# Crossing the row halves of half of the heads in a fused attention and expert kernel

## The chip, the cores and the metric

The kernel runs on one core of a Trainium2 chip. The metric is the device time of one execution in microseconds. A core has five engines with queues of their own: TensorE (PE) multiplies matrices and writes its results to PSUM banks, VectorE (DVE), ScalarE (ACT) and GpSimd (POOL) work element by element, and SyncE (SP) issues the transfers here. PE alone writes banks; POOL doesn't read them.

## The reference

Attention with gates, a recurrence over 768 steps for 2 batches of 8 heads with 40 channels each, and behind it two expert layers:

```
m_new = max(f_gate[t] + m, i_gate[t])
f, i  = exp(f_gate[t] + m - m_new), exp(i_gate[t] - m_new)
C = f * C + i * outer(v[t], k[t])          # per head 40 x 40
n = f * n + i * k[t]
y[t] = sigmoid(o_gate[t]) * (C @ q[t]) / max(|n . q[t]|, 1)
...
x1 = ((x @ w_a) * (x @ w_b)) @ w_out       # 1536 x 320, inner 1536
x2 = leaky(x1 @ w_in) @ w_out2             # inner 2048, slope 0.01
```

Inputs of the attention are single precision; the weights come as double precision and are decoded on the chip.

## The kernel before, in words

The recurrence is worked out in six chunks of 128 steps (`p` from 0 to 5) for each batch (`b`), and each chunk in two halves of 64 steps (`c`). On the partitions lie the 128 steps of a chunk; 64 u and up are the heads 4u to 4u+3 where channels lie on the partitions. For each (p, b) PE makes

- `dmm` (`decay_mm`, L341): the decays of chunk 0 and 1 spread over the partitions,
- `smm` (`score_mm`, L379): keys times queries, 16 small matmuls,
- `stm` (`state_mm`, L493): keys times values, 16 small matmuls, emptied by `ste` (L506, L508),
- `av` (`value_mm`, L436): scores times values, 32 matmuls of 64 rows by 32 columns,
- `qc` (`query_mm`, L450): queries times state, 16 matmuls of 64 by 64, onto the same two banks,
- `xmm` (L519): the transposes to the layout of the expert layer.

Each matmul in single precision is two instructions in the trace. Between them stand DVE (`dsc` the scan of the decays, L354; `sat` scores times decays, L385; `ste`; `onm`, `nrm`), POOL (`val`, `vo` values times gate; `key`; `qry`; `stk` the fading state, L499; `og`), and ACT (`sig` the sigmoid, `oab`, `nd`, `xh`). The small results (`pa`) have two banks, the `up` results (`mm`) two, the `dn` results four, which `p` = 0 borrows for scores and outputs.

The first expert layer runs on blocks of 256 tokens (blocks 0 and 1) and of 512 (2 and 4). `up` (`up_mm`, L592) is 16 matmuls, `dn` (`down`, L650 to L652) is three for each 128 tokens. Between them stand `e1`, `em`, `eh`, `el` on ACT and DVE. Each of 18 pieces of its weights (`lw:0` to `lw:17`, 640 or 768 KB) is loaded into one of four tiles `y`, then decoded by `dh` and `dl` (ACT), `dm` (DVE), `dr` (ACT, rounded part) and `ds` (POOL, L249, L250, L259, remainder), which frees the tile. Two pieces of every three are for `up`, one for `dn`.

In what order the engines get their instructions is written out by hand: the text `ORDER` lists the steps by name (`up:0:3` is block 0, slice 3; `av:1:1` is p = 1, b = 1), and each step queues its instructions, transfers too, on its engines. An engine works its queue in that order and waits where an operand isn't there or a buffer isn't free. `spin` is a matmul whose result nobody reads. `ca` closes the attention's buffers; behind it come block 4 and the second expert layer (`um`, `dd`, `ym`).

Gates: `gs` is the scan for m, `gi`, `gfa`, `gfb` the differences, `gei`, `gef`, `gst` the exponentials, `gist` the transpose of the input gate to columns, `gcum` a scan of the decays inside a chunk. `sdec` and `scum` store decays in DRAM, and `lf` and `ld` load them back, spread over partitions.

Some lines that count:

```
at_t: scores, [128 (half c on partitions 64c and up), 4 heads, 64]
ps[u]: output bank of heads 4u to 4u+3, partitions = steps
value_mm:  ps[u][x, i] += at_t[p, b, u][64 c ..., i, x] . v[64 c ..., 4 u + i]   with u = (j // 4 + c) % 2
query_mm:  ps[u][64 c ..., i] += qs[64 u ..., i, 64 c ...] . state_c[64 u ..., i]
```

Of the kernel before, what the change touches and what calls it, by code (L numbers as in the profile page):

```python
# [23 lines left out]
NP = 6  # L24
T = 128
# [8 lines left out]
    lg:0 lc:0 init lw:0 lk:0:0 gs:0 spin gi:0 gfa:0 gei:0 gfb:0 spin lg:1 gst:0 gef:0 dh:0 gz:0 gs:1 gfa:1 spin idr  # L34
    spin dl:0 gfb:1 ls:0:0 gist:0 dmm:0:1 dmm:0:0 gi:1 gcum:0 lk:0:1 gs:2 spin ls:0:1 gi:2 smm:0:0 dsc:0:1 val:0:0
    gfa:2 scum:0 gei:1 key:0:1 dm:0 val:0:1 dsc:0:0 sat:0:0:0 lw:1 vo:0:1 stm:0:1 gst:1 gef:1 vo:0:0 dr:0 sig:0:0
    key:0:0 sat:0:0:1 gz:1 smm:0:1 ld:0:1 ste:0:1:0 stm:0:0 ld:0:0 sig:0:1 ds:0 dh:1 gfb:2 lw:4 sat:0:1:0 qry:0:1
    sat:0:1:1 av:0:1 gcum:1 av:0:0 dl:1 ste:0:0:0 dm:1 qc:0:1 dr:1 stk:0:1:1 qry:0:0 dh:4 oab:0:1 onm:0:1 dl:4
    qc:0:0 oab:0:0 ste:0:1:1 lw:2 nrm:0:1 onm:0:0 stk:0:0:1 dl:2 scum:1 dh:2 gst:2 dmm:1:0 lk:1:0 lw:5 nrm:0:0 gef:2
    dm:2 ds:1 gist:1 ld:1:0 spin spin spin gei:2 og:0:1 og:0:0 nd:0:0 ste:0:0:1 val:1:0 spin lw:3 dr:2 xmm:0:0  # L40
    ls:1:0 dsc:1:0 nd:0:1 lk:2:1 dm:4 spin xmm:0:1 lk:1:1 key:1:0 xh:0:0 gz:2 xh:0:1 dr:4 xl:0:0 xl:0:1 spin spin
    spin dh:3 vo:1:0 gist:2 dh:5 ds:2 up:0:0 e1:0:0 lw:6 em:0:0 stk:1:0:0 smm:1:0 sat:1:0:1 dl:3 sat:1:0:0 ds:4 dm:3
    sig:1:1 eh:0:0 dr:3 stm:1:0 spin qry:1:0 ste:1:0:0 lw:7 stk:1:0:1 el:0:0 ste:1:0:1 ls:1:1 dl:5 up:0:1 spin
    av:1:0 qc:1:0 e1:0:1 sig:1:0 dm:5 sdec:2 oab:1:0 val:1:1 dn:0:0 dr:5 nrm:1:0 ld:1:1 dl:6 em:0:1 dh:6 ds:3 vo:1:1
    lw:9 ds:5 onm:1:0 gcum:2 dh:7 dl:7 dmm:1:1 spin up:0:3 dsc:1:1 dm:6 smm:1:1 dr:6 sat:1:1:0 og:1:0 up:0:2 eh:0:1
    sat:1:1:1 key:1:1 lw:8 stk:1:1:0 stm:1:1 dm:7 dr:7 el:0:1 lk:2:0 e1:0:3 ste:1:1:0 dl:9 e1:0:2 ds:6 stk:1:1:1
    nd:1:0 dn:0:1 em:0:3 sig:2:1 ste:1:1:1 ls:2:0 em:0:2 scum:2 lw:10 up:0:4 av:1:1 eh:0:3 eh:0:2 dl:8 qry:1:1 dh:8
    el:0:2 e1:0:4 em:0:4 qc:1:1 ld:2:1 oab:1:1 nrm:1:1 onm:1:1 ds:7 dn:0:2 eh:0:4 og:1:1 dm:8 xmm:1:0 xh:1:0 up:0:5
    nd:1:1 el:0:3 xmm:1:1 ld:2:0 val:2:0 dn:0:3 vo:2:1 xh:1:1 xl:1:0 dh:10 e1:0:5 qry:2:0 lf:2:1 lf:2:0 dr:8
    stk:2:0:0 xl:1:1 up:1:2 em:0:5 dl:10 vo:2:0 eh:0:5 ls:3:0 dh:9 dsc:2:0 key:2:0 el:0:4 e1:1:2 el:0:5 smm:2:0  # L50
    up:1:1 lw:11 sig:2:0 em:1:2 sat:2:0:1 up:1:0 dh:11 val:2:1 sat:2:0:0 dm:10 ds:8 lf:3:0 stm:2:0 dm:9 ste:2:0:0
    e1:1:0 em:1:0 ls:2:1 eh:1:2 dr:9 lf:3:1 dn:0:4 dn:0:5 eh:1:0 stk:2:0:1 ste:2:0:1 av:2:0 qc:2:0 el:1:2 stk:2:1:0
    dsc:2:1 e1:1:1 dr:10 nrm:2:0 em:1:1 up:1:5 oab:2:0 key:2:1 eh:1:1 lw:12 smm:2:1 dl:11 dl:12 el:1:1 up:1:3
# [24 lines left out]
    onm:5:1 nrm:5:1 key:5:0 stm:5:0 stk:5:0:0 ste:5:0:0 av:5:0 qc:5:0 em:2:10 oab:5:0 onm:5:0 up:2:11 el:2:9 nrm:5:0
    og:5:0 nd:5:0 og:5:1 nd:5:1 e1:2:11 xmm:5:1 xmm:5:0 xh:5:0 eh:2:10 xh:5:1 dn:2:8 em:2:11 el:2:10 xl:5:0 xl:5:1
    ca lw:19 lw:20 dn:2:9 up:4:0 e1:4:0 dh:19 eh:2:11 lw:21 em:4:0 el:2:11 up:4:1 dn:2:10 dn:2:11 dh:20 eh:4:0 dl:19  # L80
    dl:20 e1:4:1 dm:20 el:4:0 em:4:1 dm:19 eh:4:1 dr:19 up:4:2 e1:4:2 dh:21 dr:20 ye:2 dl:21 ds:19 ds:20 lw:25 lw:18
# [43 lines left out]
def attention_experts_kernel(ctx: ExitStack, tc: tile.TileContext, gates, consts, stk, kvo, w1, wd1, w2, wd2, out):  # L125
# [38 lines left out]
    ct = [[c_p.tile([128, 4, E1], F32, name=f"ct{b}{k}") for k in range(2)] for b in range(B)]  # L164
    cm = [c_p.tile([128, 4, E1], F32, name=f"cm{b}") for b in range(B)]
# [24 lines left out]

    def load_decay_f(p, b):
        t = a_p.tile([128, H, HT], F32, tag="pp", name="pp", bufs=3)
        for c in range(2):
            sp.dma_start(
                out=t[HT * c:HT * c + HT], in_=fdr[2 * p + c, b * H:b * H + H].partition_broadcast(HT)
            )
        p_t[p, b] = t

    def load_decay_c(p, b):
        t = db_free.pop(0)  # L200
        uses["db", p, b] = 2 if p in (0, NP - 1) else 3
        for u in range(2):
            h = b * H + 4 * u
            sp.dma_start(out=t[64 * u:64 * u + D], in_=ddr[p, h:h + 4].partition_broadcast(D))
        db_t[p, b] = t
# [114 lines left out]
    def gate_ist(cc, n):  # L320
        ps = ps_att("mm")
        r = slice(0, B * H)
        for j in range(n):
            pe.transpose(ps[:, j * 16:j * 16 + 16], g_i[r, (cc + j) * T:(cc + j + 1) * T], ident_all[r, 0:16])
        dve.tensor_copy(istn[:, cc:cc + n, :], ps[:, 0:n * 16].rearrange("p (c r) -> p c r", r=16))
# [10 lines left out]
    def decay_mm(p, b):  # L336
        src = ps_att()
        for h in range(H):
            row = b * H + h
            for c in range(2):  # L340
                pe.matmul(  # L341
                    src[HT * c:HT * c + HT, h * HT:h * HT + HT],
# [475 lines left out]
```

## Time and profile before

| what | value |
| --- | --- |
| time of the runs shown, median of 3 | 456.22 us (455.21 to 458.44) |
| the profiled execution, its own time | 456.19 us |
| its span, first to last instruction | 454.4 us |
| mean granted TensorE clock | 0.989 |
| busy PE, DVE, ACT, POOL | 436.2, 189.0, 213.4, 135.7 us |
| instructions of PE | 4238 matmuls and as many weight loads |
| read from and written to HBM | 39.04 and 2.05 MB |

Busy is the time in which an engine has an instruction at work; matmuls overlap, so PE can be busy and yet not at its full pace. The pace is seen in the distance from one matmul's start to the next one's. The span begins with the first instruction; what lies around it, 1.8 us here, belongs to the time but not to the profile.

### The profile page before, as it was taken

How to read it: one execution, taken by the hardware profiler on the slowest of the kernel's cores; microseconds unless marked ns; L12 is line 12 of the kernel's file. 1: busy time of each engine (PE TensorE's matmuls, PEld its weight loads, DVE VectorE, ACT ScalarE, POOL GpSimd, SP SyncE). 2: the span in 40 equal slices, each digit the busy share in tenths (PEclk: the TensorE clock that was granted, in tenths of full speed). 3: DMA queues.
4: the chain of work that ended last, by engine and by line, in shares of the span. 5: the costliest groups of instructions: out<-in, count | busy, mean ns of one | idle time of the engine just before them, and what ended most of it. 6: DMA issues, size and time to landing. Idle time of an engine off the chain costs nothing.

```text
span 454.4 us, 9997 instructions
## 1 busy us (share of the span) xinstructions
PE 436.2 (96%) x4238; PEld 388.6 (86%) x4238; DVE 189.0 (42%) x339; ACT 213.4 (47%) x412; POOL 135.7 (30%) x148
## 2 busy tenths in 40 slices
PE   6599999999999989999999999999999999999996
PEld 4568899998988877788888888989899999899896
DVE  5656687867435322243155431342431131131112
ACT  4687665576323212125676655853443343333222
POOL 6977966767410603010314241020300000000000
PEclk9978999999999999999999999999999999999999
DMA  7897675862311000015422534020010000010001
GB/s 228 272 296 236 237 235 174 270 194 77 112 55 58 1 16 1 1 40 239 138 61 66 178 90 153 0 59 0 1 58 2 0 1 0 1 58 1 0 1 58
DMA packets 12605, 41.74 MB, mean 92 GB/s; under 512 B 1904, under 2 KB 3696, under 8 KB 12560
## 3 DMA queue, kind: packets, MB, share of 16 engines
q1 hardware_dynamic: 12560, 41.10, 28.0%
q8 instruction: 33, 0.54, 0.5%
q14 instruction: 12, 0.10, 0.1%
HBM read 39.04 MB, written 2.05 MB: 90 GB/s over the span
## 4 chain that ended last, share of the span: by engine, by line
PE 84%; DMA 5%; DVE 4%; ACT 2%; issue 2%; POOL 2%; SPq 0%; POOLq 0%; DVEq 0%; ACTq 0%
PE mm L592 26%; PE mm L619 20%; PE dn L650 11%; PE dn L652 10%; PE dn L651 10%; DMA ddr<-wd 2%; DMA stk<-stk 2%; PE pa L436 2%; PE pa L493 1%; PE pa L450 1%; DMA y<-w 1%; PE pa L379 1%; PE pa L682 1%; ACT y L231 1%; PE pa L519 1%
## 5 line engine op out<-in xcount | busy, mean ns | idle before, releaser
L592 PE MATMUL mm<-xh,wa 128*128 128x256 f32 (+1 forms) x480 | 117.3, 345 | 0.6 <-POOL wa L250 0.6
L592 PEld LDWEIGHTS mm<-xh,wa 128*128 128x128 f32 x480 | 80.6, 192 | 9.8 <-POOL wa L250 0.8
L592 PE MATMUL mm<-xl,wa 128*128 128x256 f32 (+1 forms) x288 | 80.0, 339 | 0.0
L635 DVE TENSOR_TENSOR gl<-gg,gh 128x512 fp32r<-128x512 f32 x48 | 34.2, 731 | 99.4 <-ACT gh L630 95.2
L625 ACT ACTIVATE gg<-mm 128x512 f32<-128x512 f32 x48 | 28.1, 593 | 72.3 <-PE mm L619 69.6
L650 PE MATMUL dn<-wa,gh 128*128 128x320 f32 x192 | 59.6, 310 | 0.0
L652 PE MATMUL dn<-wa,gl 128*128 128x320 f32 x192 | 59.4, 309 | 0.0
L651 PE MATMUL dn<-wa,gh 128*128 128x320 f32 x192 | 59.3, 309 | 0.0
L592 PEld LDWEIGHTS mm<-xl,wa 128*128 128x128 f32 x288 | 51.9, 192 | 5.8
L602 DVE TENSOR_TENSOR gg<-gg,mm 128x256 f32<-128x256 f32 (+1 forms) x48 | 26.3, 550 | 66.5 <-PE mm L592 30.4
L597 ACT ACTIVATE gg<-mm 128x256 f32<-128x256 f32 (+1 forms) x48 | 23.2, 486 | 57.3 <-PE mm L592 50.2
L650 PE MATMUL dn<-wd,gh 128*128 128x320 f32 x144 | 46.3, 322 | 0.0
L652 PE MATMUL dn<-wd,gl 128*128 128x320 f32 x144 | 44.6, 309 | 0.0
L651 PE MATMUL dn<-wd,gh 128*128 128x320 f32 x144 | 44.5, 309 | 0.0
L611 DVE TENSOR_TENSOR gl<-gg,gh 128x256 fp32r<-128x256 f32 (+1 forms) x48 | 35.5, 745 | 11.0 <-ACT gh L606 10.6
L630 ACT ACTIVATE gh<-gg 128x512 fp32r<-128x512 f32 x48 | 29.8, 630 | 21.7 <-PE dn L651 21.3
L606 ACT ACTIVATE gh<-gg 128x256 fp32r<-128x256 f32 (+1 forms) x48 | 25.0, 524 | 27.1 <-DVE gg L602 15.8
L651 PEld LDWEIGHTS dn<-wa,gh 128*128 128x128 f32 x192 | 36.1, 188 | 1.2
L650 PEld LDWEIGHTS dn<-wa,gh 128*128 128x128 f32 x192 | 36.1, 188 | 1.2
L652 PEld LDWEIGHTS dn<-wa,gl 128*128 128x128 f32 x192 | 36.0, 188 | 0.0
L619 PE MATMUL mm<-yh,wa 128*128 128x512 f32 x120 | 35.8, 396 | 0.0
L619 PE MATMUL mm<-yh,w 128*128 128x512 f32 x120 | 35.6, 394 | 0.0
(114 smaller groups left out, 702.8 us busy)
## 6 DMA issues: line engine op xcount, KB each, us to landing
y<-w SPq DMA_DIRECT2D x12, 768.0 KB
raw<-w SPq DMA_DIRECT2D x8, 768.0 KB
kvo<-kvo SPq DMA_DIRECT2D x12, 484.0 KB
raw<-wd SPq DMA_DIRECT2D x8, 640.0 KB
stk<-stk SPq DMA_DIRECT2D x24, 160.0 KB
y<-wd SPq DMA_DIRECT2D x6, 640.0 KB
pp<-fdr SPq DMA_DIRECT2D x16, 128.0 KB
db<-ddr SPq DMA_DIRECT2D x24, 80.0 KB
```

The source lines that it names most:

```text
L592: pe.matmul(halves_[ab], w[:, slot, ab, :], xs[lo][:, kt, cs], start=i == 0, stop=i == 7)
L597: act.activation(out=g, in_=up_t[blk, f][0], func=AF.Copy)
L602: dve.tensor_tensor(out=g, in0=g, in1=up_t.pop((blk, f))[1], op=ALU.mult)
L606: act.activation(out=gh, in_=g_t[blk, f], func=AF.Copy)
L611: dve.tensor_tensor(out=gl, in0=g_t.pop((blk, f)), in1=raw_view(gh_t[1, blk, f]), op=ALU.subtract)
L619: pe.matmul(ps, w[:, slot, f % 2, :], xs[lo][:, kt, :], start=i == 0, stop=i == 7)
L625: act.activation(out=g, in_=ps, func=AF.Prelu, alpha=0.01)
L630: act.activation(out=gh, in_=g_t[2, blk, f], func=AF.Copy)
L635: dve.tensor_tensor(out=gl, in0=g_t.pop((2, blk, f)), in1=raw_view(gh_t[2, blk, f]), op=ALU.subtract)
L650: pe.matmul(ps, gh[:, cs], w[:, 0, :], start=f == 0, stop=False)
L651: pe.matmul(ps, gh[:, cs], w[:, 1, :], start=False, stop=False)
L652: pe.matmul(ps, gl[:, cs], w[:, 0, :], start=False, stop=f == last)
```

## The change

Keys and values of the heads 4 to 7 are laid out with the two halves of a chunk swapped on the partitions (on the host, `crossed`); decays, gate columns and scores of these heads follow. Wherever a row half of 64 partitions was half `c`, it is `c ^ u` now. So the value groups can use four different tiles of 64 by 64, and have 16 matmuls in place of 32. Because value and query group then write some of the same places from different row halves, a new step `sy` reads one element of the output bank between them. The gate rows are sorted by (u, b, head), the gate columns come from matmuls with ones on a diagonal in place of transposes, decays are stored with four transfers in place of one, and in the tile `kvo` the output gates stand behind the values. `ORDER` up to `ca` is another; from `ca` on it is the same.

```
-ORDER: lg:0 lc:0 init lw:0 lk:0:0 gs:0 spin gi:0 ... (to ca)
+ORDER: lg:0 lc:0 init gs:0 gi:0 gfa:0 gfb:0 spin gei:0 lk:0:1 ... (to ca)
 loads before:  lg:0 lc lw:0 lk:0:0 lg:1 ls:0:0 lk:0:1 ls:0:1 scum:0 lw:1 ld:0:1 ld:0:0 lw:4 lw:2 scum:1 lk:1:0 lw:5 ld:1:0 lw:3 ls:1:0
 loads after:   lg:0 lc lk:0:1 lk:0:0 lg:1 lw:0 ls:0:1 scum:0 ls:0:0 ld:0:1 lw:1 ld:0:0 lw:2 lk:1:0 scum:1 lw:4 lw:3 ld:1:0 lw:6 ls:1:0
 ACT before:    gei:0 gst:0 gef:0 dh:0 idr dl:0 gei:1 gst:1 gef:1 dr:0 sig:0:0 sig:0:1 dh:1 dl:1 dr:1 dh:4 oab:0:1 dl:4 oab:0:0 dl:2 dh:2
                gst:2 gef:2 gei:2 nd:0:0 dr:2 nd:0:1 xh:0:0 xh:0:1 dr:4 dh:3 dh:5 e1:0:0 dl:3 sig:1:1 eh:0:0 dr:3
 ACT after:     gei:0 gst:0 gef:0 gst:1 gef:1 gei:1 idr dh:0 dl:0 dr:0 gst:2 gef:2 gei:2 sig:0:0 dh:1 dl:1 dl:2 oab:0:0 dr:1 dh:2 sig:0:1
                oab:0:1 sig:1:0 dr:2 dh:4 dl:4 nd:0:0 dh:3 nd:0:1 dr:4 dl:3 xh:0:1 xh:0:0 dl:6 dr:3 dh:6 e1:0:0 e1:0:3 eh:0:0
 PE before:     up:0:0 smm:1:0 stm:1:0 spin up:0:1 spin av:1:0 qc:1:0 dn:0:0 dmm:1:1 spin up:0:3 smm:1:1 up:0:2 stm:1:1 dn:0:1 up:0:4 av:1:1
 PE after:      up:0:0 smm:1:0 up:0:3 stm:1:0 up:0:1 av:1:0 qc:1:0 up:0:2 dn:0:0 stm:1:1 up:0:4 smm:1:1 dn:0:1 av:1:1
 PE before:     smm:5:0 up:2:10 smm:5:1 dn:2:6 stm:5:1 av:5:1 qc:5:1 dn:2:7 stm:5:0 av:5:0 qc:5:0 up:2:11
 PE after:      smm:5:0 dn:2:0 stm:5:0 dn:2:1 av:5:0 up:2:4 qc:5:0 ... smm:5:1 dn:2:3 stm:5:1 dn:2:4 av:5:1 up:2:7 qc:5:1
@@ load_decay_f
-                out=t[HT * c:HT * c + HT], in_=fdr[2 * p + c, b * H:b * H + H].partition_broadcast(HT)
+                out=t[HT * c:HT * c + HT].rearrange("p (u i) t -> p u i t", u=2),
+                in_=fdr[2 * p + c].rearrange("(u b i) t -> b u i t", u=2, b=B)[b].partition_broadcast(HT),
@@ store_decays
-        sp.dma_start(
-            out=fdr[lo // HT:hi // HT].rearrange("c r t -> r c t"),
-            in_=g_e[:, lo:hi].rearrange("r (c t) -> r c t", t=HT),
-        )
+        for c in range(2):
+            src = g_e[:, lo:hi].rearrange("r (p c t) -> r p c t", c=2, t=HT)[:, :, c]
+            to = fdr.rearrange("(p c) r t -> c r p t", c=2)
+            for u in range(2):
+                r = slice(8 * u, 8 * u + 8)
+                sp.dma_start(out=to[c ^ u, r, lo // T:hi // T], in_=src[r])
@@ gate_ist
-            pe.transpose(ps[:, j * 16:j * 16 + 16], g_i[r, (cc + j) * T:(cc + j + 1) * T], ident_all[r, 0:16])
+            t = (cc + j) * T
+            o = ps[:, 32 * j:32 * j + 32]
+            pe.matmul(o[:, 0:16], g_i[:, t:t + T], ident_all[0:B * H, 0:16])
+            for c in range(2):
+                pe.matmul(
+                    o[HT * c:HT * c + HT, 8:24], g_i[:, t + HT * (1 - c):t + HT * (1 - c) + HT],
+                    ident_all[0:B * H, 0:16],
+                )
@@ score_mm, state_mm (r = half(c ^ u)), decay_mm
-                    pe.matmul(sc_t[p, b, u][ts, i * HT:i * HT + HT], x[:, 1, i, ts], x[:, 0, i, ts])
+                    pe.matmul(sc_t[p, b, u][half(c ^ u), i * HT:i * HT + HT], x[:, 1, i, ts], x[:, 0, i, ts])
@@ value_mm
-        for j in range(8):
-            for c in range(2):
-                u, i = (j // 4 + c) % 2, j % 4
-                for w in (2 * c, 2 * c + 1):
-                    x = slice(32 * w, 32 * w + 32)
+        for i in reversed(range(4)):
+            for u in (1, 0):
+                for c in range(2):
+                    r = half(c ^ u)
                     pe.matmul(
-                        ps[u][x, i], at_t[p, b, u][HT * c:HT * c + HT, i, x.start - HT * c:x.stop - HT * c],
-                        v[HT * c:HT * c + HT, 4 * u + i, :],
-                        start=fresh(seen, (u, w)), stop=True, skip_group_check=True,
+                        ps[u][half(c), i], at_t[p, b, u][r, i], v[r, 4 * u + i, :],
+                        start=fresh(seen, (u, c)), stop=True, skip_group_check=True,
                     )
+
+    def rows_apart(p, b):
+        ps, seen = out_banks(p, b)
+        dve.tensor_copy(apart[p * B + b][HT:HT + 1], ps[0][HT:HT + 1, 0, 0:1])
```

The new step's name in `ORDER` is `sy`; on DVE `sy:1:0` stands behind `dm:5`, `sy:0:0` behind `gcum:2`. The exponentials `gst:2 gef:2 gei:2` are those of the gates of the chunks 2 to 5.

## Rows read from the trace of the kernel before

**Rows 1.** The page's first and fourth section: busy time, and the chain by engine.

```profile
PE 436.2 (96%) x4238; PEld 388.6 (86%) x4238; DVE 189.0 (42%) x339; ACT 213.4 (47%) x412; POOL 135.7 (30%) x148
...
PE 84%; DMA 5%; DVE 4%; ACT 2%; issue 2%; POOL 2%; SPq 0%; POOLq 0%; DVEq 0%; ACTq 0%
```

**Rows 2.** Stretches: busy us (instructions) by engine, granted clock, DMA share, GB/s.

```profile
20.00:30.00 10.00, 7.41 (x64) 4.85 (x63) 5.68 (x16) 8.06 (x19) 7.11 (x10) 0.66 0.90 299
...
50.00:60.00 10.00, 9.44 (x159) 8.95 (x158) 5.17 (x14) 6.66 (x18) 9.04 (x11) 1.00 0.59 192
...
36.00:38.00 2.00, 2.00 (x12) 2.00 (x11) 0.90 (x3) 2.00 (x4) 1.60 (x3) 0.53 0.89 354
```

**Rows 3.** The chain that ended last, in order of time: start us, us, what.

```profile
36.12 3.32 PE mm L592 x16
...
42.56 0.85 DVE wd L310
...
53.23 0.74 PE pa L436 x64
53.97 0.61 PE pa L450 x32
...
59.10 1.99 PE mm L592 x16
61.10 0.62 PE pa L379 x32
...
65.75 0.61 PE pa L493 x32
```

**Rows 4.** Timeline of PE, a `dn` and the value group behind it.

```profile
78.51 0.31 PE L651 MATMUL dn<-wd,gh 128*128 128x320 f32 x1
78.66 0.31 PE L652 MATMUL dn<-wd,gl 128*128 128x320 f32 x1
78.90 0.81 PE L436 MATMUL pa<-kvo,at 64*32 64x41 f32 x64
```

**Rows 5.** Timeline of PE: the first `up`, and the last `decay_mm`.

```profile
30.50 0.74 PE L592 MATMUL mm<-xh,wa 128*128 128x256 f32 x4
...
42.19 1.15 PE L341 MATMUL pa<-wd,ident 16*64 16x64 f32 x32
```

**Rows 6.** Groups by line and form: busy us, mean ns, idle us before.

```profile
L227 ACT ACTIVATE y<-y 128x768 f32<-128x768 f32 x12 | 10.9, 916 | 4.1 <-DMA y<-w 4.1
...
L385 DVE TENSOR_TENSOR at<-pa,pp 128x256 f32<-128x256 f32 x20 | 7.7, 416 | 10.3 <-PE pa L379 10.2
```

**Rows 7.** The largest waits of PE, 36 to 205 us: us in total, times, longest.

```profile
PE pa L436 <- DVE cm L508: 1.1, 3, 0.5
PE pa L493 <- DVE at L385: 0.9, 1, 0.9
PE pa L519 <- POOL ya L480: 0.8, 1, 0.8
PE pa L436 <- DVE ct L508: 0.6, 1, 0.6
PE mm L592 <- POOL wa L250: 0.6, 1, 0.6
```

**Rows 8.** Timeline at 164 us: a state's add, and the value group that waits.

```profile
164.30 0.33 DVE L508 TENSOR_TENSOR cm<-pa,cm 128x164 f32<-128x164 f32 x1 [1.37 <-PE pa L493]
...
164.69 0.27 PE L436 MATMUL pa<-kvo,at 64*32 64x41 f32 x4 [0.51 <-DVE cm L508]
```

**Rows 9.** Timeline of SP's queue: the load `ld:1:0`.

```profile
23.60 0.68 SPq L204 DMA_DIRECT2D db<-ddr  x2
```

**Rows 10.** Timeline of ACT in the start-up.

```profile
25.30 1.28 ACT L294 ACT_TABLE_LOAD   x1
...
28.88 0.46 ACT L533 ACTIVATE xh<-pa 128x384 fp32r<-128x384 f32 x1
...
34.58 1.28 ACT L410 ACT_TABLE_LOAD   x1
```

More of the change, by code (lines that the diff above doesn't have):

```diff
@@ L33 @@
 ORDER = """
[L34 to L53, printed above, removed]
@@ L79 @@
-    og:5:0 nd:5:0 og:5:1 nd:5:1 e1:2:11 xmm:5:1 xmm:5:0 xh:5:0 eh:2:10 xh:5:1 dn:2:8 em:2:11 el:2:10 xl:5:0 xl:5:1
-    ca lw:19 lw:20 dn:2:9 up:4:0 e1:4:0 dh:19 eh:2:11 lw:21 em:4:0 el:2:11 up:4:1 dn:2:10 dn:2:11 dh:20 eh:4:0 dl:19
-    dl:20 e1:4:1 dm:20 el:4:0 em:4:1 dm:19 eh:4:1 dr:19 up:4:2 e1:4:2 dh:21 dr:20 ye:2 dl:21 ds:19 ds:20 lw:25 lw:18
+    lg:0 lc:0 init gs:0 gi:0 gfa:0 gfb:0 spin gei:0 lk:0:1 spin spin spin spin gs:1 gst:0 gi:1 lk:0:0 gfa:1 gfb:1
+    spin lg:1 gef:0 gz:0 gst:1 spin lw:0 ls:0:1 gef:1 spin gist:0 spin gcum:0 spin gz:1 val:0:1 gei:1 scum:0 idr
@@ new lines @@
+    val:0:0 ls:0:0 vo:0:1 dh:0 gcum:1 ld:0:1 dmm:0:0 gs:2 lw:1 gfa:2 dsc:0:0 dmm:0:1 dsc:0:1 dl:0 ld:0:0 gist:1 spin
+    key:0:0 smm:0:1 lw:2 lk:1:0 dm:0 key:0:1 vo:0:0 stm:0:1 smm:0:0 gfb:2 sat:0:1:0 sat:0:1:1 av:0:1 dr:0 gst:2 ds:0
+    qry:0:1 gi:2 gef:2 gei:2 gz:2 sig:0:0 sat:0:0:0 stm:0:0 ste:0:0:0 qry:0:0 stk:0:0:1 sat:0:0:1 av:0:0 scum:1
+    ste:0:1:0 gcum:2 lw:4 dmm:1:1 dh:1 dl:1 sy:0:1 stk:0:1:1 sy:0:0 qc:0:0 dl:2 oab:0:0 dm:1 dr:1 dsc:1:1 onm:0:0
+    dh:2 ste:0:1:1 ste:0:0:1 qc:0:1 val:1:0 ds:1 sig:0:1 lw:3 dm:2 nrm:0:0 oab:0:1 ld:1:0 sig:1:0 onm:0:1 dr:2 dh:4
@@ new lines @@
+    lw:6 ls:1:0 gist:2 dmm:1:0 dl:4 ld:1:1 og:0:0 nd:0:0 nrm:0:1 xmm:0:0 spin vo:1:0 spin og:0:1 dm:4 spin dh:3
+    dsc:1:0 ds:2 nd:0:1 lw:5 dr:4 dl:3 spin xmm:0:1 xh:0:1 ds:4 spin dm:3 xh:0:0 dl:6 lk:1:1 lw:7 xl:0:1 dr:3 xl:0:0
+    dh:6 up:0:0 dm:6 smm:1:0 up:0:3 key:1:0 sat:1:0:1 e1:0:0 sdec:2 e1:0:3 scum:2 ds:3 em:0:0 eh:0:0 dr:6 sat:1:0:0
+    stm:1:0 up:0:1 dh:5 stk:1:0:0 qry:1:0 ste:1:0:0 dl:5 stk:1:0:1 ds:6 ls:1:1 el:0:0 em:0:3 ste:1:0:1 key:1:1
+    val:1:1 sig:1:1 dm:5 av:1:0 sy:1:0 dh:7 vo:1:1 lw:11 qc:1:0 eh:0:3 dl:7 el:0:3 e1:0:1 up:0:2 stk:1:1:0 dn:0:0
@@ L164, in attention_experts_kernel @@
     ct = [[c_p.tile([128, 4, E1], F32, name=f"ct{b}{k}") for k in range(2)] for b in range(B)]
+    apart = [c_p.tile([128, 1], F32, name=f"apart{n}") for n in range(NP * B)]
     cm = [c_p.tile([128, 4, E1], F32, name=f"cm{b}") for b in range(B)]
@@ L189, in load_kvo, with row @@
         kvo_t[p, b] = t
+    def row(b, h):
+        return h // 4 * 8 + b * 4 + h % 4
     def load_decay_f(p, b):
@@ L202, in load_decay_c @@
         for u in range(2):
-            h = b * H + 4 * u
-            sp.dma_start(out=t[64 * u:64 * u + D], in_=ddr[p, h:h + 4].partition_broadcast(D))
+            r = row(b, 4 * u)
+            sp.dma_start(out=t[64 * u:64 * u + D], in_=ddr[p, r:r + 4].partition_broadcast(D))
         db_t[p, b] = t
@@ L367, in attention_experts_kernel, with half @@
     sc_t = {}
+    def half(c):
+        return slice(HT * c, HT * c + HT)
     def score_mm(p, b):
@@ L421, in out_banks, with fresh @@
         return [pv for _, _, pv in o_t[p, b]], begun[p, b]
-    def fresh(seen, *keys):
-        new = not seen & set(keys)
-        seen |= set(keys)
+    def fresh(seen, key):
+        new = key not in seen
+        seen.add(key)
         return new
@@ L451, in query_mm @@
                         ps[u][x, i], qs_t[p, b][r, i, x], st[c][r, i, :],
-                        start=fresh(seen, (u, 2 * c), (u, 2 * c + 1)), stop=True, skip_group_check=True,
+                        start=fresh(seen, (u, c)), stop=True, skip_group_check=True,
                     )
@@ L491, in state_mm @@
                 for c in range(n):
-                    r = slice(HT * c, HT * c + HT)
+                    r = half(c ^ u)
                     pe.matmul(ps[c][64 * u:64 * u + 64, i], kvo_t[p, b][r, h * D:h * D + 64], v[r, h, :])
@@ L773 @@
     q, k, v, og = (np.asarray(inputs[n]) for n in ("q", "k", "v", "o_gate"))
-    fg = np.asarray(inputs["f_gate"]).reshape(B * H, S)
-    ig = np.asarray(inputs["i_gate"]).reshape(B * H, S)
+    fg, ig = (
+        np.asarray(inputs[n]).reshape(B, 2, 4, S).transpose(1, 0, 2, 3).reshape(B * H, S) for n in ("f_gate", "i_gate")
+    )
     NC = S // T
@@ L785, in nat, with crossed @@
         return x.reshape(B, H, NC, T, D).transpose(0, 2, 3, 1, 4)
+    def crossed(x):
+        y = nat(x).copy()
+        y[:, :, :, 4:] = np.roll(y[:, :, :, 4:], HT, axis=2)
+        return y
     kvo = np.zeros((B, NC, T, KVO), np.float32)
-    kvo[..., 0:NK] = nat(k).reshape(B, NC, T, NK)
-    kvo[..., NK:2 * NK] = nat(og).reshape(B, NC, T, NK)
-    kvo[..., 2 * NK:].reshape(B, NC, T, H, E1)[..., 0:D] = nat(v)
+    kvo[..., 0:NK] = crossed(k).reshape(B, NC, T, NK)
+    kvo[..., NK + NV:] = nat(og).reshape(B, NC, T, NK)
+    kvo[..., NK:NK + NV].reshape(B, NC, T, H, E1)[..., 0:D] = crossed(v)
     dup = np.concatenate([np.arange(320), np.arange(256, 320)])
```

90 lines of the change are left out of this document (53 added, 37 removed).

## The prediction, made before the changed kernel was run

> **What bounds the kernel now.** I read the page's first sections first: TensorE (PE) is busy for 96% of the span and the chain that ended last is PE for 84% [rows 1]. A busy PE is not a PE at its peak, so I next read stretches of ten microseconds [rows 2]. Between 20 and 30 us PE is busy for 7.4 of 10, while the transfers take 0.90 of the sixteen engines' time; from 60 us on PE waits only briefly [rows 7]. So there are two kernels in one: a start-up in which PE waits for loads, gates and decoded weights, and a long stretch in which it streams expert matmuls. After the step `ca` the order is unchanged, so whatever the change gains or loses before it is carried one to one to the end, as long as PE stays the last to finish.
>
> How fast PE streams comes from the chain in order of time [rows 3]: an `up` of 256 columns takes 1.99 us, a group of scores 0.62, of states 0.61, of values 0.74, of queries 0.61. A `dn` is six matmuls 0.15 apart; where a value group follows, the distance is 0.24, so each entry into such small tiles costs 0.09 us [rows 4]. All this is at the full clock.
>
> How much PE loses in the start-up: `up:0:0` starts at 30.50 [rows 5] and the value group `av:1:1` at 53.23 [rows 3], 22.7 us apart. In between lie five `up` (10.0), two score and two state groups (2.5), a value and a query group (1.35), two `dn` (1.8), a `decay_mm` (1.15, [rows 5]) and five entries (0.45): 17.2 us at full pace. So 5.5 us are lost there. One piece shows: `up:0:1` takes 3.32 instead of 1.99, in a stretch with a granted clock of 0.53, behind waits for scores and states [rows 2, 3]. From 36 to 205 us PE's waits with a named releaser are 4.0 us in their five largest rows [rows 7]; the value groups have 1.7 of it, because they stand right behind state groups, whose two banks must first be emptied.
>
> **The change part by part.**
>
> *Value tiles.* A value group goes from 32 matmuls of 64x32 to 16 of 64x64; each is two instructions in the trace, so 64 become 32. The nearest rows are the query and the state group, which have the form to come: 32 instructions of 64x64 in 0.61 us [rows 3]. That saves 0.74-0.61 = 0.13 us, twelve times: -1.6 us. The bounds are -1.6 and 0 (if the new tiles don't run side by side as those of the query group do).
>
> What speaks against this part: until now, whenever two row halves of the array work at once, they write different banks (scores and queries: bank by row half; states: bank by `c`; values: `u = (j//4+c)%2`). After it both row halves write one bank in neighbouring matmuls, in the value and state groups, though other partitions of it. The Trainium skill has a rule against that (TensorEngine Tiling (Array Packing), Restrictions and Gotchas, the first gotcha): different row tiles cannot access the same PSUM bank at the same time. No row of before can show it; it is a rival below.
>
> *The order on PE.* Before, a query group stands right behind its value group; after, a `dn` or `up` lies between, except for `av:1:0` and `qc:1:0`. From `up:0:0` on I count 27 stretches of small tiles in the old order and 39 in the new one: 12 more entries of 0.09 us [rows 4], +1.1 us (bounds 0 and 2.2). So the first two parts nearly cancel.
>
> *The new wait `sy`.* A VectorE (DVE) copy of one element reads bank 0 after the value group, and the query group may write there only after that. Nothing hides that where `qc` stands directly behind: `av:1:0`. There the copy is queued on DVE behind the merge `dm:5`, which itself waits for ScalarE's (ACT) decode; behind the query group on PE stand all later `up` steps. Elsewhere a `dn` or `up` of 0.9 us or more covers it, which is gone if DVE is late. No such copy is in the trace. The nearest is a value group that waits 0.51 us for a DVE add of 0.33 [rows 8]; without the add's length 0.2 is left. I take 0.7, that round and some 0.5 of a merge that is not done; bounds 0.2 and 4 (a late DVE in half of the chunks).
>
> *Gate columns.* Six transposes become 18 single-precision matmuls, 36 instructions. At `decay_mm`'s 1.15/32 = 0.036 us [rows 5] they are 1.3 us. They lie in the start-up, where PE waits anyway: 0; 1.3 if all of it is on the path.
>
> *Stores and loads of decays.* `sdec` becomes four DMAs, three more issues of 0.34 us on SyncE's (SP) queue, if they cost what the loads of `ddr` do (two in 0.68, [rows 9]); the broadcasts come in pieces half as long. Behind them on SP stand `ls:1:1` and weights that are used later: 0, bounds 0 and 1.
>
> *The start-up order.* All exponentials (`gst:2 gef:2 gei:2`) move ahead of the first sigmoid. So the third and fourth table load, 1.28 us each at 25.30 and 34.58 [rows 10], should go; the one stands ahead of `nd:0:0` and `xh:0:0`, the other ahead of `eh:0:0` and `dr:3`. Against that `dh:3 dl:3` are put ahead of `xh`, two of 0.92 us [rows 6]: together +0.5 us for `xh:0:0`, which is at 28.88 now [rows 10]. And `lw:0` moves from third to sixth among the loads, behind 1.0 MB more, 3.4 us at 299 GB/s [rows 2], which delays the first decode; ACT waited for other things afterwards, so little of it should arrive at `xh`. I let `up:0:0` start where it did, give or take 2 us. What differs is behind it: `up:0:3` follows with its weights decoded, one table load fewer delays `eh:0:0`, `decay_mm` of chunk 1 is already done (1.15 us out of this stretch), and the long scan `gcum:2`, in the chain at 42.56 [rows 3], moves to a time before the first query group. I take 4.0 of the 5.5 us as recovered; bounds: -7.5 (all, and a start 2 us sooner) and +2 (none, and a start 2 us later).
>
> *Waits from 60 to 205 us.* In the new order a `dn` or an `up` lies between state and value group, and between scores and values, in chunks 2 to 5. That takes away the 1.7 us before the value groups and most of the 0.9 before a state group [rows 7]; with the matmuls behind them that start late some 3.3. Where only a `dn` of 0.9 lies between scores and values (`smm:3:0`, `smm:4:1`), two products of 0.42 us [rows 6] must fit in it: 0.6 comes back. -2.7; bounds -4.0 and +2.
>
> **The sum** against the profiled execution: 454.4 -1.6 +1.1 +0.7 -4.0 -2.7 = 447.9. That execution took 456.2, 1.8 more than its span, which is also the median of the runs: 447.9 + 1.8 = 449.7.
>
> **The rivals.**
>
> *The stalls come back elsewhere.* Weights are ready only just in time: one `up` waits 0.6 us for GpSimd's (POOL) remainder [rows 7], and POOL is busy for 9.0 of 10 us from 50 to 60 [rows 2]. If PE runs 4 us ahead it may run into POOL instead. Then of the two gains (4.0 and 2.7) little stays, say 1: 454.4 -1.6 +1.1 +0.7 -1 = 453.6, and 1.8, so 455.4, within 453 and 459. For it speaks POOL's load; against it, that POOL is idle for 2.9 of 10 us from 20 to 30 [rows 2].
>
> *Slower: one bank from two row halves.* If such pairs run one after the other, value and state groups have half as many tiles at a time. The nearest row is `decay_mm`, all in one row group: 1.15 for 32 instructions against 0.61 [rows 3, 5], +0.54 us for 24 groups = 13.0: 449.7+13.0 = 462.7. It decides as soon as both groups take more than 0.9 us each in the trace. By that rule of the Trainium skill this is what happens. That the partitions differ speaks against it.
>
> *The start-up moves as a whole.* If loads come early and ACT hardly waits, `up:0:0` starts 2 us sooner and all 5.5 are recovered: 449.7-3.5 = 446.2, and with all later waits gone 444.9; 442 to 446.
>
> *The value group does not get shorter* (0.74 stays): 451.3, inside the first case.
>
> **Chances.** The forecast, 446 to 453: 0.52. Stalls elsewhere, 453 to 459: 0.28. One bank: 0.10. The start-up as a whole: 0.08; something unseen and slower: 0.02. The range from 444 to 458 holds the first, nearly all of the second and half of the early start; 0.17 is left out. A measurement of this kernel tells about 1% (4.6 us) from no change. Faster by over 1% (below 451.7) is most of the first case and the early start: 0.5. Slower (above 460.8) is the bank case and the unseen: 0.12. Within: 0.38.
>
> **What would show it.** Right: value groups of 32 instructions in about 0.61 us; two table loads fewer on ACT; `av:1:1` reached near 49 us instead of 53.23; waits of PE after 60 us under 2 us, none before a query group over 0.3 but at `qc:1:0`. Wrong: PE waiting for POOL's `wa` between 40 and 120 us (stalls elsewhere); value or state groups over 0.9 us (one bank); query groups that wait for DVE in several chunks, which would put the new wait's price above 0.7; `up:0:0` after 32.5.

## The result, and the profile after

The changed kernel takes 451.2 us (median of 11 runs, 449.1 to 454.5), the kernel before 456.2 (11 runs, 455.2 to 458.7): a ratio of 0.989, 95% interval 0.985 to 0.993. The forecast was 449.7. The profiled execution of the changed kernel took 454.5, the longest of its runs, where that of before took 456.2. TensorE's granted clock rises late in it (at 36.8 us, see the end of this section); a third trace, further below, shows a run in which it rises early (at 30.7).

The page's first and fourth section again:

```profile
PE 442.1 (98%) x3884; PEld 391.5 (86%) x3884; DVE 196.0 (43%) x351; ACT 209.5 (46%) x410; POOL 137.9 (30%) x148
...
PE 88%; DMA 3%; DVE 3%; ACT 2%; issue 2%; SPq 1%; POOL 1%; DVEq 0%; POOLq 0%; ACTq 0%
```

PE has 354 instructions fewer than in [rows 1] (384 fewer for the value tiles, 30 more for the gate columns) and is busy for longer: the first sign that a busy PE is not one that does more. Two table loads of ACT are gone, as the two that are left show (groups by line, with their count, busy us, mean ns):

```profile
L297 ACT ACT_TABLE_LOAD x1 | 1.3, 1283 | 3.1 <-DMA wd<-gates 3.1
L433 ACT ACT_TABLE_LOAD x1 | 1.3, 1283 | 0.0
```

The value group, in the timeline of PE (start us, us, what), beside a `dn`, as in [rows 4]:

```profile
102.59 0.31 PE L676 MATMUL dn<-wd,gh 128*128 128x320 f32 x1
102.73 0.31 PE L677 MATMUL dn<-wd,gl 128*128 128x320 f32 x1
102.97 0.68 PE L458 MATMUL pa<-kvo,at 64*64 64x41 f32 x32
103.58 0.74 PE L617 MATMUL mm<-xh,wa 128*128 128x256 f32 x4
```

From the group to the next step are 0.61 us for 32 instructions, 0.74 for 64 before; the entry still costs 0.24-0.15 = 0.09. So the new tiles run side by side as those of the query group do, and both row halves of the array write one bank, in different partitions, at no loss. The Trainium skill (TensorEngine Tiling (Array Packing), Restrictions and Gotchas) states that different row tiles cannot access the same PSUM bank at the same time. This trace shows no cost of that: the prediction, from this case's rows, had put the group at over 0.9 us if such pairs ran one after the other.

The waits of PE from 36 to 205 us (us in total, times, longest), beside those of [rows 7]:

```profile
PE pa L475 <- DVE apart L465: 2.3, 2, 1.6
PE pa L544 <- ACT ya L537: 0.7, 1, 0.7
PE pa L518 <- issue: 0.6, 1, 0.6
PE pa L398 <- DVE ct L533: 0.5, 1, 0.5
```

The sum is 4.1, as before, but the rows are others: the value groups' 1.7 are gone, and the query groups wait 2.3 for the new copy. The timeline of DVE at those two places shows who holds the copy up:

```profile
42.23 1.67 DVE L241 SCALAR_TENSOR_TENSOR y<-y 128x640 int32<-128x640 int32 x1 [0.87 <-ACT y L237]
43.94 0.16 DVE L465 COPY apart<-pa 1x1 f32<-1x1 f32 x1
...
73.37 2.33 DVE L241 SCALAR_TENSOR_TENSOR y<-y 128x768 int32<-128x768 int32 x1
75.62 0.41 DVE L627 TENSOR_TENSOR gg<-gg,mm 128x256 f32<-128x256 f32 x1
76.06 0.16 DVE L465 COPY apart<-pa 1x1 f32<-1x1 f32 x1
```

`sy:1:0` could begin when `av:1:0` ends, at 42.6, and begins at 43.94, behind a merge of 1.67 us; `sy:2:0` stands behind one of 2.33. The mean of these two forms is 1.20 and 1.24 us, and both long ones lie beside GpSimd's products from their first moment to their last. The copy itself takes 0.16.

The first `up`, which started at 30.50 [rows 5], in the timeline of PE:

```profile
32.51 1.22 PE L617 MATMUL mm<-xh,wa 128*128 128x256 f32 x4 [0.53 <-ACT xh L558]
33.53 0.73 PE L617 MATMUL mm<-xl,wa 128*128 128x256 f32 x2
...
36.32 0.58 PE L398 MATMUL pa<-stk 40*64 40x64 f32 x10
```

It starts 2.0 us later and takes 3.81 us to the next step in place of 2.12: four of its matmuls take 1.22 where four took 0.74. So it runs at the lower of the clock's two levels (1.2 and 2.4 GHz). This trace holds no record of the granted clock before 36.8 us; there the record sets in, at the full clock.

### The profile page after: what moved, and what is told of

It reads as the page before. It is cut to its first block, busy times and chain, and to the rows that moved or that the text cites. A ratio compares the mean times of both kernels' runs of the same rounds, so it can differ in the third digit from the quotient of the medians.

```text
span 452.8 us, 9327 instructions
## 1 busy us (share of the span) xinstructions
PE 442.1 (98%) x3884; PEld 391.5 (86%) x3884; DVE 196.0 (43%) x351; ACT 209.5 (46%) x410; POOL 137.9 (30%) x148
## 4 chain that ended last, share of the span: by engine, by line
PE 88%; DMA 3%; DVE 3%; ACT 2%; issue 2%; SPq 1%; POOL 1%; DVEq 0%; POOLq 0%; ACTq 0%
PE mm L617 29%; PE mm L644 20%; PE dn L675 11%; PE dn L677 11%; PE dn L676 11%; DMA y<-wd 2%; DMA y<-w 1%; PE pa L398 1%; PE pa L475 1%; PE pa L544 1%; PE pa L458 1%; PE pa L518 1%; DVE y L241 1%; PE pa L707 1%; DVE pp L370 1%
## 5 line engine op out<-in xcount | busy, mean ns | idle before, releaser
L676 PEld LDWEIGHTS dn<-wa,gh 128*128 128x128 f32 x192 | 36.1, 188 | 1.3
L631 ACT ACTIVATE gh<-gg 128x256 fp32r<-128x256 f32 (+1 forms) x48 | 24.9, 522 | 25.3 <-DVE gg L627 17.6
```

Of the source, the lines that this page charges most:

```text
L631: act.activation(out=gh, in_=g_t[blk, f], func=AF.Copy)
L676: pe.matmul(ps, gh[:, cs], w[:, 1, :], start=False, stop=False)
```

## The experiments

Every ratio is to runs of the kernel before on the same chip. One run of the order alone, of 1461.5 us, is left out of its numbers. "The stretch" is the time from the start of `up:0:0` to that of `up:4:0`, behind which nothing changes.

**The changed kernel again**, for its spread.

> The changed kernel once more, for its spread: its runs lie between 449.1 and 454.5, and the profiled one, at 454.5, is the slowest of them. If the spread comes from the start-up (my theory), this profile shows the same distances between steps from the first up of chunk 0 on as the first profile, and another start of up:0:0 or another granted clock before 40 us; the time then differs by that. If it comes from waits spread over 40 to 200 us (rival), up:0:0 starts at 32.5 again and the difference grows later. Ratio to the kernel before 0.985 to 0.993 by both.

452.15 us (449.94 to 454.02, 4 runs), ratio 0.989 (0.983 to 0.996). Its trace, of 453.87 us, repeats the first one: clock record from 36.7 us, `qc:1:0` 1.69 us late, `qc:2:0` 0.84 (0.73 beyond the entry, which the prediction prices apart). As both traces are of long runs, this does not decide between the two texts. The fifteen runs so far fall into two groups, 449 to 451.2 and 453.2 to 454.5.

**The order alone**: the code of before with the new `ORDER`, without its `sy`.

> The code of the kernel before with the new order, without the step sy (values in 64x32 tiles, old layout, transposes). If the order is what gains (my theory), and the two waits for sy (1.7 and 0.8 us) and the longer gate columns cost, this is faster than the changed kernel by 1 to 2.5 us, although each value group takes 0.13 us longer (+1.6): ratio to before 0.983 to 0.989. If the tiles are what gains (rival), it is level with the kernel before: 0.997 to 1.003.

453.55 us (452.07 to 454.73), ratio 0.993 (0.991 to 0.996). That lies between the two texts: the order brings a part of the gain, and not more than the whole change does. The stretch is 167.4 us, against 174.5 before and 170.9 in the changed kernel, and without the copy none of its query groups waits. But part of this difference is the clock, which was up here before `up:0:0` began (2.57 us, against 3.81). From `av:3:0` to `up:4:0`, where the order is the same, its value groups of 0.74 make 101.35 us, the changed kernel's of 0.61 make 100.46: 0.15 for each of six. Its start-up is later (`up:0:0` at 34.8), behind a stop of PE of 2.4 us inside a `decay_mm` at 20.9 us, put down to issue alone; whether the other runs have that stop is not known.

**The tiles alone**: the new code in the old order, with each `sy` right behind its `av`.

> The changed code with the old order; each sy stands right behind its value group, so that ten query groups wait for DVE with nothing between on PE. By my theory value tiles save 1.6 us and each uncovered wait costs 0.35 us at least and over 1 us where DVE has a longer step in hand: 10 x 0.35 to 10 x 1.2 = 3.5 to 12 us, so 458 to 467, ratio 1.004 to 1.023, and value groups of 0.61 us. If the wait were cheap (rival: under 0.15 us each), 454.5 to 456, ratio 0.997 to 1.0.

465.61 us (462.32 to 467.36), ratio 1.018 (1.011 to 1.025): slower than before. The waits of PE from 36 to 205 us:

```profile
PE pa L474 <- DVE apart L464: 3.4, 10, 0.5
PE pa L457 <- DVE cm L532: 1.5, 3, 0.5
```

All ten query groups wait for the copy, and value groups still wait for state adds as in [rows 7]. The distance from a value group to its query group is 1.05 us in five of the ten places, 0.44 more than the group's own 0.61, and 0.95 and 1.19 in two. It is 1.7 to 1.8 for `av:4:1`, `av:5:0` and `av:5:1`, but not because DVE is busy: there the value group itself stands for the state's add after its first matmuls, and the copy follows at once, as in the timeline of the trace

```profile
196.82 0.66 PE L457 MATMUL pa<-kvo,at 64*64 64x41 f32 x28 [0.50 <-DVE cm L532]
197.53 0.16 DVE L464 COPY apart<-pa 1x1 f32<-1x1 f32 x1 [0.77 <-PE pa L457]
```

So an uncovered copy costs 0.44, more than the 0.13 that the tiles save, and the new tiles are worth nothing without the new order; the 1 us and more that the text allowed for a busy DVE is not seen here. Of the 6.0 us by which this trace reaches `up:4:0` later than before, 2.3 lie ahead of `up:0:0`: `gist:2` stands right ahead of it there, and takes 2.45 us in place of 0.35.

**The copies earlier**: in `ORDER` of the changed kernel

```diff
- ... val:1:1 sig:1:1 dm:5 av:1:0 sy:1:0 dh:7 ...
+ ... val:1:1 sig:1:1 av:1:0 sy:1:0 dm:5 dh:7 ...
- ... em:1:2 e1:1:3 dm:9 em:1:3 ds:14 sig:2:0 dr:9 eh:1:3 dn:1:1 sy:2:0 eh:1:2 qc:2:0 ...
+ ... em:1:2 sy:2:0 e1:1:3 dm:9 em:1:3 ds:14 sig:2:0 dr:9 eh:1:3 dn:1:1 eh:1:2 qc:2:0 ...
```

> The changed kernel with two steps of DVE moved: the merge dm:5 behind sy:1:0, and sy:2:0 ahead of the merge dm:9 and the product em:1:3. If the waits at qc:1:0 (1.7 us) and qc:2:0 (0.8 us) are lost time on the path (my theory), both fall to 0.4 us or less and the time falls by 1.5 to 2.2 us against the changed kernel: ratio to before 0.981 to 0.987. If PE then waits for the weights of that merge or for the product instead (rival), the two waits fall, others of the same length appear within 15 us behind them, and the ratio stays 0.987 to 0.991.

450.52 us (449.89 to 451.49, 4 runs), ratio 0.987 (0.980 to 0.993). The waits of PE from 36 to 205 us:

```profile
PE pa L517 <- POOL wa L255: 1.2, 1, 1.2
PE pa L543 <- ACT ya L536: 0.7, 1, 0.7
PE pa L474 <- DVE apart L464: 0.4, 1, 0.4
```

`qc:1:0` waits 0.44 and `qc:2:0` not at all; the state group `stm:2:1` waits for POOL instead, and loses 1.27 where it lost 0.68 (without the entry). The ratio lies where the two texts meet, so the time alone does not decide. The wait between the two output products (L543, ACT's copy into `ya`) is that of the changed kernel.

**Four questions to the start-up.** First the matmuls of a gate-column group sorted by shape, all full ones and then all halves:

> The changed kernel with the matmuls of each gate-column group in another order: all full ones (16 rows by 128) first, then all halves (16 rows by 64), in place of one full and two halves by turns. In the changed kernel the third group, 4 full and 8 halves, took 3.35 us where the 4 full ones alone took 1.1 before. If each change between a 128-wide and a 64-wide tile costs time, one change is left of eight, and the group takes 1.5 to 2.4 us. If the halves cost this by themselves (single precision at the lower clock), it stays at 3.2 to 3.4. By both the time of the whole stays within 1 us of the changed kernel, since the first output product behind the group waits for GpSimd's gated rows until 27.6 us in any case; if the group was on the path, it gains 1 to 1.5.

452.84 us (450.98 to 453.94), ratio 0.988 (0.983 to 0.992): as the changed kernel. (The 1.1 us in that text are the three groups of before together; its third, of four transposes, takes 0.35, from 30.15 to 30.50.) In the timeline of PE the third group is

```profile
22.48 1.88 PE L333 MATMUL mm<-ident,wd 16*128 16x16 f32 x8
24.29 1.04 PE L338 MATMUL mm<-ident,wd 16*64 16x16 f32 x16
25.17 1.10 PE L361 MATMUL pa<-wd,ident 16*64 16x64 f32 x16
```

2.69 us in place of 3.35. So neither range is met, and both theories hold a part: about 0.7 us came from the order of the shapes, and four full matmuls and eight halves still take 2.7. Of those 0.7 nothing arrives: `up:0:0` starts at 31.8.

Next the load of the first weight words put third (`lw:0` ahead of `gs:0`):

> The changed kernel with the load of the first weight words put third among the loads, where the kernel before has it. The first decoding step on VectorE began at 10.5 us in the changed kernel and at 6.6 before. If that late load is why the first up group came 2.0 us later than before (32.5 against 30.5), the first decoding step begins near 6.6 again, the first up group at 30.5 to 31.5, and the whole gains 1 to 2 us. Rival: the first up group waits for the chain through attention, normalisation and GpSimd's gating, which begins with the loads of keys, values and queries; these then land later by the time of one load, the first up group stays at 32 or moves to 33, and the time is the same or up to 1 us longer.

456.17 us (452.86 to 458.62, 10 runs), ratio 0.996 (0.993 to 0.999): the gain is nearly gone. The first decoding step (it is ACT's) begins at 6.66 us instead of 10.52, and `up:0:0` at 32.7. The rival was right, and by more than its price: a state group now waits 2.42 us, until 14.94, for keys and gates on POOL. This trace is of the fastest of the ten runs; what the median loses beyond it, 3.3 us, is not in it.

Then the third gate-column group moved behind `smm:1:0`, six fills (`spin`) in its place:

> The changed kernel with the third gate-column group moved behind the first score group of the second chunk, and six filling matmuls in its place. Theory: the low granted clock until 36.8 us in the profiled execution is what keeps the start-up from its forecast gain, and dense filling work in place of the twelve small single-precision matmuls lets the clock rise sooner. Then the clock rises by about 30 us, the first up group takes 2.4 in place of 3.8 us, the second value group of the second chunk begins near 49 to 51 in place of 53.1, and the time is 449 to 451 in every run. Rival: the clock in the start-up does not depend on these; it rises anywhere from 30 to 37, and the runs spread from 449 to 454.5 as those of the changed kernel do.

457.38 us (455.42 to 459.11, 10 runs), ratio 0.999 (0.996 to 1.002): as before the change. Neither text's time is met. The clock was up at 31.7, but the group took 2.6 us where nothing else could go, `up:0:3` behind it 3.6, and the clock fell again. So the move put a new loss on the path, and whether an early clock alone brings the forecast gain is not decided by it. Here are the stretches (busy us and instructions of PE, PEld, DVE, ACT, POOL; granted clock, DMA share, GB/s):

```profile
34.00:36.00 2.00, 2.00 (x45) 1.80 (x43) 1.03 (x1) 0.85 (x2) 1.84 (x3) 1.00 1.00 399
...
38.00:40.00 2.00, 1.67 (x10) 1.63 (x9) 1.22 (x4) 0.00 (x0) 0.89 (x1) 0.64 0.66 212
46.00:50.00 4.00, 3.05 (x48) 3.03 (x49) 2.85 (x6) 2.08 (x5) 3.94 (x5) 0.85 0.77 229
```

Last the four fills between `xmm:0:0` and `xmm:0:1` left out, with both `xh` of ACT ahead of `dr:4 dl:3` (and `dm:3` behind them):

> The changed kernel without the four filling matmuls that its order puts between the two first output products, and with ScalarE's two copies of the second product set ahead of two decoding steps. In the third trace of the changed kernel the first product begins at 27.4 us, where the kernel before has it at 27.7, but the second at 29.8 against 28.9, behind four fills of 0.43 us each, and the first up group at 31.6 against 30.5. If these fills and the two steps on ScalarE are the delay, the second product begins near 28.3, the first up group at 30.0 to 30.5, and the time falls by 1 to 1.5 us. Rival: the fills also keep TensorE's granted clock rising; without them it rises later than 30.7, the up groups of the start-up take longer than 2.4 us each, and the time is the same or up to 4 us longer.

457.75 us (455.17 to 458.25, 10 runs), ratio 1.000 (0.997 to 1.002): the whole gain is lost, 5 to 6 us, where the rival allowed up to 4. In the timeline of PE

```profile
29.42 0.87 PE L542 MATMUL pa<-ident,ya 128*128 128x128 f32 x3 [1.14 <-DVE pp L368]
...
31.25 1.23 PE L615 MATMUL mm<-xh,wa 128*128 128x256 f32 x4 [0.54 <-ACT xh L556]
34.76 0.79 PE L615 MATMUL mm<-xl,wa 128*128 128x256 f32 x2 [2.29 <-DVE xl L562]
```

`xmm:0:1` starts at 29.42 and not at 28.3, because what the fills had covered becomes a wait for DVE; and inside `up:0:0` PE waits 2.29 us for `xl`, because my move also put the merge `dm:3`, ahead of `xl` on DVE, behind two more steps of ACT. The granted clock is 0.50 in all the stretches from 30 to 38 us and rises at 39.3. So this run shows what a stop in the start-up costs, but not the fills by themselves.

**A third trace of the changed kernel.**

> The changed kernel once more, for another trace of it. If the spread of its runs (449.1 to 454.5) comes from where the granted clock rises in the start-up, the rise and the length go together: a rise near 30 us with about 450, one near 37 with about 454. If the clock does not set it, the length and the rise are unrelated, and the traces differ elsewhere, behind 60 us.

452.64 us, with the clock up at 30.7. `up:0:0` starts at 31.6 and takes 2.5 us, `av:1:1` starts at 49.15 (53.06 in the first trace), and `qc:1:0` waits only 0.44, as the merge `dm:5` had run at 39.78, before `av:1:0` ended. An early rise with 452.6 us fits neither text as it stands. Without one stop of some 2.1 us, in the timeline of PE inside `dn:0:2`, it would have been near 450.5 (an estimate):

```profile
50.01 0.31 PE L676 MATMUL dn<-wd,gh 128*128 128x320 f32 x1
52.18 0.31 PE L677 MATMUL dn<-wd,gl 128*128 128x320 f32 x1 [1.86 <-DVE y L241]
```

The merge that is named ended at 51.33, and the weight load of PE shows 2.0 us of issue there. No other trace has this stop; it is not explained.

**The copy on ACT** instead of DVE (`act.copy` in `rows_apart`).

> The changed kernel with the one-element copy between value group and query group on ScalarE in place of VectorE. In the traces of the changed kernel the query groups wait for it behind value groups: 1.69 us at the first half of the second chunk or 2.13 at its second half, and 0.84 in the third chunk, each time with a merge of the weight decoding of 1.7 to 2.3 us ahead of the copy on VectorE. If VectorE's queue is the price, the waits fall to 0 to 0.5 each where ScalarE is free, 1.5 to 2.5 us in sum, and the time to 449 to 450. Rival: ScalarE is as full there (decoding steps of 0.9 us each); waits of 0.5 to 1.5 come in other places, and the time stays at 451 to 453.

451.54 us (450.07 to 455.48, 4 runs), ratio 0.987 (0.983 to 0.992): as the changed kernel. (The 2.13 us of that text were the stop inside `dn:0:2`, and not a wait for the copy; I had misread them.) `qc:1:0` waits 0.43 now, but `qc:2:0` 1.62, since ACT is no freer:

```profile
75.26 0.90 ACT L250 ACTIVATE wa<-y 128x768 fp32r<-128x768 f32 x1 [1.81 <-DVE y L241]
76.06 0.40 ACT L631 ACTIVATE gh<-gg 128x256 fp32r<-128x256 f32 x1
76.48 0.15 ACT L465 COPY apart<-pa 1x1 f32<-1x1 f32 x1
```

The copy waits behind a decoding step that itself waits for DVE's merge. The rival was right; the engine is not the price, the place in its queue is. Right behind that stop the granted clock fell once more (0.57 from 78 to 82 us), which no trace of the changed kernel shows; this trace is of the longest of the four runs.

**More covers**: the earlier copies, `up:0:2` ahead of `qc:1:0`, `dn:0:3` between the output products of chunk 1, `stm:2:1` behind `dn:1:2`, and the gate columns sorted.

> The version with the one-element copies early (two merges behind them), with three more covers: an up group of 2.0 us between the first value and query group of the second chunk, a down group between that chunk's two output products (1.0 us lost there), and another ahead of a state group of the third chunk (0.8 to 1.4 lost); the gate-column matmuls are sorted by shape. If each of these losses is a wait that work in front can fill, the first up group to the first of the last up groups takes 165 to 166.5 us in place of 167.7, and the time is 447.5 to 449.5. Rival: the groups that were moved come to wait themselves for ScalarE's and VectorE's steps, or push the wait to the next group; the stretch stays at 167 to 169 and the time at 450 to 451.

453.17 us (452.48 to 456.36, 11 runs), ratio 0.993 (0.990 to 0.995). The waits of PE from 36 to 205 us:

```profile
PE pa L400 <- DVE ct L535: 1.4, 1, 1.4
PE pa L546 <- ACT ya L539: 0.7, 1, 0.7
PE dn L679 <- DVE gl L638: 0.7, 1, 0.7
```

The wait at `qc:1:0` is gone; 1.4 us before a score group and 0.7 before a `dn` have come, and the output product waits its 0.7 as before. The stretch is 171.2 us, and the clock rises late in this trace (36.1 us). The version without these covers needs 168.9 with a late clock (the next run), so they cost 2.3 us: the rival, and worse.

**The earlier copies once more**, the text of "the copies earlier" unchanged.

> The version with the two one-element copies early once more, the text unchanged. From the first up group to the first of the last up groups its first trace took 167.7 us, the third trace of the changed kernel 169.9 with the same clock and the waits 0.44, 2.13 and 0.84 us for the copy. If these waits were the only difference and belong to the order, the trace shows 167.7 again where the clock rises near 30 us and near 169.1 where it rises near 37, with no query group waiting over 0.5, and the median lies 1 to 2.5 us below the 451 to 452 of the changed kernel's runs. Rival: the gain of the first measurement was the clock that it happened to meet; then the runs spread from 449 to 454 with a median of 451 to 452.

451.05 us (450.14 to 451.62, 6 runs), ratio 0.987 (0.983 to 0.991). This trace has the late clock (36.2 us, `up:0:0` takes 3.8 us) and still needs only 168.9 us for the stretch, against 170.9 and 171.2 in the two traces of the changed kernel with the late clock; no query group waits over 0.44. So the order does save 2 us there, as the text said (169.1). Where the clock is early it saves little: 167.7 against 169.9, of which 2.1 are the unexplained stop. The ten runs of this version lie between 449.9 and 451.6, sixteen of the changed kernel between 449.1 and 454.5. The medians are 451 and 452; the intervals of the two ratios overlap, so no gain is shown beyond the narrower spread.

The mean granted clock of the runs without a trace bears on this. In some runs the record holds the low stretch too, and its mean tells how long that was: 0.974 goes with a rise at 31.8 us (`lw:0` third), 0.970 with one at 36.1 (more covers). Of the first eleven runs of the changed kernel, the three with 0.972 or 0.973 took 449.1 to 451.2 us, the three with 0.970 took 453.2 to 453.6. With the earlier copies, the one with 0.973 took 450.8, the two with 0.969 took 451.0 and 451.1. So, as far as the six runs that tell it go, the two groups go with the time of the rise, and the earlier copies take most of that away.

## Why the prediction was right, and where its steps were not

The total came out as forecast, 1.5 us from it. The steps behind it did less well, and some of the nearness is luck.

- *Value tiles, -1.6.* Right: 0.74 to 0.61 in the trace, and 0.15 a group between the order alone and the changed kernel. The rival of one bank is refuted.
- *Entries, +1.1.* The price holds: the median `up` ahead of such a group lasts 2.10 us to the next step where others last 2.01, and a `dn` 1.07 against 0.98. The count was made on the orders and is the same.
- *The copy, +0.7.* Mis-sized. It cost 1.69+0.73 = 2.4 us in the two traces with the late clock and 0.44+0.73 = 1.2 in the early one. The place was right (`qc:1:0`), and also the reason, a merge that is not done; but a second place, `qc:2:0`, lost its cover because a merge took 2.33 us there. The bounds of 0.2 and 4 held.
- *Gate columns, 0.* The groups take 5.1 us and not 1.3, as 0.036 us an instruction came from `decay_mm`, half as wide, without changes of shape, and at the full clock; the third group takes 3.35 us in the start-up and 2.6 at the full clock (in the run that moved it). They were indeed off the path where the new order has them, as far as the sorted version shows: 0.7 us less of them changed nothing. In the old order, right ahead of `up:0:0`, they are on it.
- *Start-up, -4.0 with `up:0:0` unmoved.* Mis-sized, and not as one number. From `up:0:0` to `av:1:1` were 22.7 us; after, 17.6 with the early clock (-5.1) and 20.6 or 20.8 with the late one (-2.0). And `up:0:0` itself came 1.1 to 2.0 later. The net is -4.0 with the early clock and -0.1 or -0.7 with the late one. What I took for stalls to be filled is for a good part the granted clock: the two traces with the late clock lose 1.4 us in `up:0:0`, 1.25 more at `qc:1:0` and 0.8 behind `smm:1:1`, and win back 0.6 behind `stm:1:0`. Only the first of these is the clock itself; the others are waits that came with it. In sum they are 3.0 and 3.2 us longer to `av:1:1`, nearly the distance of the two groups of runs, and the mean clocks of the runs agree; but it is not shown by a run in which the clock alone differs.
- *`lw:0` late and unimportant.* Right: earlier, it made the kernel slower.
- *Waits from 60 us, -2.7.* Those ahead of value and state groups in chunks 3 to 5 are gone; after 80 us PE loses nothing over 0.3 at any step, where before it lost 5 us from 100 us on. Against that stand 0.7 at `qc:2:0`, 0.7 at `stm:2:1` and 1.0 between two output products, so the sign "no query group waits over 0.3 but `qc:1:0`" did not hold. From `av:1:1` to `up:4:0` the kernel gained 151.8-150.4 = 1.4 us; of the -2.8 that the prediction's terms make there (nine twelfths of the tiles, all entries, all of this term) that is half.
- *The condition "stalls elsewhere".* In part true, not with POOL but with DVE and the copy. The profiled execution (454.5) lies in that rival's range, and its `up:0:0` at 32.51 just meets the sign "after 32.5"; but by the above the late clock has the larger part in it, which is not that rival's mechanism. The faster half of the runs lies in the forecast's range.

So, as far as the traces go, the forecast was met because its largest term is right in the faster runs: -4.0 to `av:1:1` and -1.4 behind it make -5.4, against a forecast of -6.5. In the slower ones it misses by what the copy and the late first `up` add; the first trace gains only 1.5 us to `up:4:0`. That enough runs met the early clock to put the median near the forecast is luck: the prediction said nothing of where the clock would rise. And no trace of the changed kernel is of one of its faster runs: their account is that of the third trace less its stop, and of the version with the earlier copies.

## What to carry to other kernels

Price a new one-element wait by what stands ahead of it in the queue of its engine, not by its own length: here 0.16 us became 0.44 uncovered and 1.7 behind a merge, and moving it up saves 2.0 to 2.3 us of the stretch in the traces with the late clock, more than the tiles that it was for. Take the tiles and the order as one change: the order alone gave 0.993, the tiles alone 1.018, both 0.989 (the intervals of the first and the last just touch). Before you fill, sort or advance anything in a start-up, ask what will stand still for it, and what clock the next long group will then have: three sensible improvements here cost 4 to 6 us.

## What the runs showed of the hardware that was not expected

- Two row halves of the array writing one bank in different partitions run at full pace (0.61 us for 32 instructions of 64x64, in value and state groups).
- Alternating between 16x128 and 16x64 tiles in single precision took 3.35 us for 24 instructions, sorted 2.69, both before the clock's rise; alternating at the full clock it took 2.6.
- The merges on DVE (18 of 128x640 and 128x768) take 0.80 us at the least, 1.07 in the median and 2.33 at the most. In all fourteen traces together, 247 merges (those of the second layer's weights counted too) have nothing running on POOL beside them, and they take 0.81 to 0.96 us; every merge over 0.97 us has POOL at work beside it for some of its time, though many others beside POOL are no longer than these. That points to POOL's work as what made the merge long and the copy late; no run here takes it away.
- The same text meets a clock that rises at 30.7, 36.7 or 36.8 us, and so an `up` of 2.5 or 3.7 to 3.8 us at the same place. In three versions with longer stops of PE behind it, it fell again: 0.64 from 38 to 40 us and 0.85 from 46 to 50 (third gate-column group late), 0.57 from 46 to 50 (fills left out), 0.57 from 78 to 82 (copy on ACT). Before the change it fell too, to 0.57 from 36 to 40.
- PE stopped for 2.0 and 2.4 us in two traces with no releaser that fits, inside `dn:0:2` and inside a `decay_mm`; this stays open.
